# Batch 0's early attention pairs: v pooled by GpSimd, the pooled result kept on chip, key rows through DRAM left out

## The chip, the cores and the metric

The kernel runs on one core of a Trainium2 chip. The metric is the time of one execution in microseconds (us), and smaller is better. The engines are named as in the profile: PE multiplies matrices (its weight load is PEld), DVE and ACT are the vector and the scalar engine, POOL is GpSimd, and SP issues the transfers.

## What is computed

```python
# q, k, v: (8 batches, 8 heads, 576 positions, 64)
q_d, k_d, v_d = (t.reshape(B, H, 144, 4, D).mean(axis=3) for t in (q, k, v))
out_up = np.repeat(softmax(q_d @ k_d.T / 8) @ v_d, 4, axis=2)
mask = abs(i - j) < 4
out_local = softmax(where(mask, q @ k.T / 8, -1e9)) @ v
x = (out_up + out_local) as (batch, 576 positions, 512 channels)
u = x + ((x.T @ U @ V).T)              # U 576x32, V 32x576
out = u + relu(u @ w_ch1) @ w_ch2      # 512 -> 2048 -> 512
```

Two attentions are added: one over positions averaged in fours, whose result each position of a four receives, and one over a band of seven neighbours. A product of rank 32 mixes the positions, and a feed-forward part (FFN) follows. U, V and the two weight matrices arrive as 64-bit floats; the kernel splits each into a high and a low part, and each FFN product is three matrix products (high by high, high by low, low by high).

## The kernel before

The attention is cut into 32 pairs, a batch and two of its heads; pair n is heads 2(n mod 4) and the next one of batch n div 4. The FFN is cut into 256 steps: 8 batches, 2 tiles of 288 positions, 16 chunks of 128 hidden channels. A step has an `ffn1` (12 matmuls, L888: u by a chunk of w1 into `ps_h`) and an `ffn2` (12 matmuls, L911: the hidden chunk by w2 into `acc`), and `ffn2` runs three steps behind. u is held for a whole batch as `uH` and `uL`, 128 channels (one pair) by 288 positions each, so the FFN of a batch starts when the u of its fourth pair is there.

There are two ways to make a pair. The first NE = 5 pairs are early: `early_global` averages q and k on POOL, averages v by matmuls with the constant matrix `pool_sb` (L427), and writes the attention over averages to DRAM (`up_e`). `load_up` brings it back into rows 38 to 45 of `vw`, the tile with v's windows for the band. `local_blocks` computes the band in blocks of 32 positions on PE; its last product (`ps_ba`, L651) multiplies `vw`, and so contains the averaged part. `early_mix` makes u from the result `ob`: `hu` (L673) multiplies it by `Ublk`, and `um` adds V's product (L688) and turns the blocks by matmuls with the identity (L690). Pair 4 is early too, but belongs to batch 1: its x goes to DRAM (L661, L662).

The other pairs are late: `late_global`, then `local_attn`, where POOL forms the products `Pt` of the band (L795; five of them for a pair, the last half as wide) from tiles `vl` that are loaded for it, and DVE sums them (L800). x goes to DRAM, `mix_part` loads it (`xL`, `Y`), and u is made of `hu` (L844), V's product (L859), `uH` on ACT (L865) and `uL` on POOL (L867).

W1 and W2 are split by `convert`, 16 chunks each: ACT (L339), three DVE instructions (L341, L343, L345), ACT for the high part (L347), POOL for the low part (L350). W2's parts lie where the early pairs' tiles were, so no W2 chunk is finished before the last early operation is done (the key "late"). `load_ublk` and `load_v` split U and V in the same way.

Nothing waits at run time except for data and buffers: `Plan` is given every operation with an assumed duration and a priority, simulates the five engines, and writes the order of each engine's instructions once. An engine then runs its instructions in that order, so an instruction that waits holds back all behind it.

## Time and profile before

| | |
|---|---|
| time, median of 3 runs | 990.95 us (990.48 to 991.46) |
| profiled execution | 992.23 us, of which its trace spans 990.4 us |
| mean granted clock of PE | 0.972 of full speed |
| busy share of the span | PE 95%, POOL 55%, DVE 52%, ACT 39% |

The span runs from the first to the last instruction of the trace; the rest of the execution's time lies around it. Busy shares are means over stages that differ, so the stages have rows of their own further down.

### The profile page before, as it was taken

Reading aid. Unit: us, or ns where it says so; the run is one execution under the profiler, and the core shown is the slowest. Engines: PE = TensorE matmul, PEld = TensorE weight load, DVE = VectorE, ACT = ScalarE, POOL = GpSimd, SP = SyncE. Lnnn points to the kernel's source line nnn. Section 1 sums busy time; section 2 is a strip of 40 time slices with the busy share of each in tenths; the row PEclk is TensorE's granted clock in tenths of the full one; section 3 lists DMA queues with packets and bytes.
Section 4 is the critical chain, followed back from the end, with each engine's and each line's share of the span. In section 5 each row is a group of like instructions: output and inputs, shape, how many; then the busy total and the mean of one; then the engine's idle time right before and its main releaser. Section 6 shows DMA issues by size and latency. Waiting matters only on the chain.

```text
span 990.4 us, 26862 instructions
## 1 busy us (share of the span) xinstructions
...
## 2 busy tenths in 40 slices
...
GB/s 263 277 137 171 204 210 92 141 144 100 142 117 123 114 109 116 150 126 123 119 111 132 106 126 111 150 126 127 124 101 135 120 109 87 105 36 25 1 25 25
DMA packets 222612, 120.30 MB, mean 121 GB/s; under 512 B 175492, under 2 KB 198456, under 8 KB 222488
## 3 DMA queue, kind: packets, MB, share of 16 engines
...
q14 instruction: 39, 0.32, 0.1%
HBM read 87.78 MB, written 30.75 MB: 120 GB/s over the span
## 4 chain that ended last, share of the span: by engine, by line
PE 81%; DVE 11%; ACT 3%; issue 2%; DMA 2%; POOL 1%; SPq 0%; DVEq 0%; ACTq 0%; POOLq 0%
PE ps_h L888 34%; PE acc L911 34%; PE ps_a L548 3%; DVE acc L800 2%; PE ps_b L715 2%; DVE c L343 2%; PE ps_hu L844 1%; DVE o L925 1%; PE ps_t L535 1%; PE ps_v L427 1%; DVE c L345 1%; PE ps_b L722 1%; PE ps_a L480 1%; DVE hL L896 1%; DVE c L341 1%
## 5 line engine op out<-in xcount | busy, mean ns | idle before, releaser
L888 PE MATMUL ps_h<-uH,W1H 128*128 128x288 f32 x1024 | 297.9, 291 | 4.7 <-DVE hL L896 4.7
L911 PE MATMUL acc<-hH,W2H 128*128 128x288 f32 x1024 | 299.8, 293 | 0.0
L888 PE MATMUL ps_h<-uL,W1H 128*128 128x288 f32 x1024 | 295.0, 288 | 0.6 <-POOL uL L867 0.6
L888 PE MATMUL ps_h<-uH,W1L 128*128 128x288 f32 x1024 | 294.8, 288 | 0.0
L911 PE MATMUL acc<-hH,W2L 128*128 128x288 f32 x1024 | 293.6, 287 | 0.7 <-POOL W2L L350 0.7
L911 PE MATMUL acc<-hL,W2H 128*128 128x288 f32 x1024 | 293.3, 286 | 0.0
L896 DVE SCALAR_TENSOR_TENSOR hL<-ps_h,hH 128x288 fp32r<-128x288 f32 x256 | 116.5, 455 | 332.4 <-ACT hH L895 331.3
L795 POOL TENSOR_TENSOR Pt<-vl,at 128x896 f32<-128x896 f32 (+1 forms) x135 | 218.9, 1691 | 114.9 <-DVE acc L800 59.1
L895 ACT ACTIVATE hH<-ps_h 128x288 fp32r<-128x288 f32 x256 | 104.8, 409 | 350.6 <-PE ps_h L888 349.0
L888 PEld LDWEIGHTS ps_h<-uH,W1H 128*128 128x128 f32 x1024 | 195.3, 191 | 7.1 <-DVE hL L896 5.8
L888 PEld LDWEIGHTS ps_h<-uL,W1H 128*128 128x128 f32 x1024 | 195.4, 191 | 0.9 <-POOL uL L867 0.9
L888 PEld LDWEIGHTS ps_h<-uH,W1L 128*128 128x128 f32 x1024 | 195.4, 191 | 0.0
L911 PEld LDWEIGHTS acc<-hH,W2L 128*128 128x128 f32 x1024 | 194.0, 189 | 1.1 <-POOL W2L L350 1.1
L911 PEld LDWEIGHTS acc<-hH,W2H 128*128 128x128 f32 x1024 | 194.1, 190 | 0.4
L911 PEld LDWEIGHTS acc<-hL,W2H 128*128 128x128 f32 x1024 | 194.1, 190 | 0.0
L800 DVE TENSOR_REDUCE acc<-Pt 128x128 f32<-128x1024 f32 (+1 forms) x135 | 146.3, 1104 | 2.3 <-POOL Pt L795 1.4
L836 POOL TENSOR_TENSOR xL<-xL,xH 116x640 fp32r<-116x640 f32 x28 | 43.3, 1547 | 110.5 <-ACT xH L835 102.1
L921 POOL TENSOR_TENSOR o<-uH,uL 128x288 f32<-128x288 f32 x64 | 49.0, 796 | 49.5 <-DMA out_t<-o 49.5
L740 ACT ACTIVATE se<-ps_b 96x114 f32<-96x114 f32 x108 | 38.4, 355 | 73.1 <-PE ps_b L715 59.9
L506 POOL TENSOR_TENSOR vr<-vr 72x256 f32<-72x256 f32 x54 | 40.6, 753 | 30.3 <-DMA vr<-in_v 30.3
L867 POOL TENSOR_TENSOR uL<-xT,uH 128x288 fp32r<-128x288 f32 x56 | 43.7, 801 | 21.3 <-ACT uH L865 21.3
L789 ACT ACTIVATE Pt<-ul 128x128 f32<-128x128 f32 (+1 forms) x135 | 46.2, 421 | 14.0 <-DVE acc L800 13.7
(126 smaller groups left out, 1091.1 us busy)
## 6 DMA issues: line engine op xcount, KB each, us to landing
...
```

What stands on the lines that cost most here:

```text
L506: pool_tt(256, lambda x=x: nc.gpsimd.tensor_tensor(out=x()[:, :, 0:2, :], in0=x()[:, :, 0:2, :], in1=x()[:, :, 2:4, :], op=ALU.add), [x], ...
L740: act(n * KL, lambda p=ps[hh], se=se, n=n, rows=rows: nc.scalar.activation(se()[rows, 0:n].rearrange("p r k -> p (r k)"), p()[rows, 0:n * ...
L789: act(n * D, lambda n=n, ps=ps, Pt=Pt: nc.scalar.activation(Pt()[:, :n, :, 7], ul()[:, ps, :], AF.Copy), [ul], [(Pt, 1)], prio, 0.16)
L795: nc.gpsimd.tensor_tensor(out=Pt()[:, :n, :, 0:7].rearrange("p s d o -> p o s d"), in0=win, in1=at()[:, ps, :].rearrange("p s o -> p o s") ...
L800: dve(8.5 * n * D, lambda n=n, ps=ps, Pt=Pt: nc.vector.tensor_reduce(out=acc()[:, ps, :], in_=Pt()[:, :n], axis=AX.X, op=ALU.add), [(Pt, 0 ...
L836: pool_tt(640, lambda: nc.gpsimd.tensor_tensor(out=xL(), in0=xL().bitcast(F32), in1=xH().bitcast(F32), op=ALU.subtract), [xL, xH], [xL], prio)
L867: pool_tt(TN, lambda uH=uH, uL=uL, uf=uf: nc.gpsimd.tensor_tensor(out=uL()[:, hp, :], in0=uf(), in1=uH()[:, hp, :].bitcast(F32), op=ALU.su ...
L888: nc.tensor.matmul(ps()[:, :TN], w[:, dc, fs], turns(u()[:, dc, :]), start=(n == 0), stop=(n == 3 * NDC - 1))
L895: last_h[i] = act(TN, lambda: nc.scalar.activation(hH(), ps()[:, :TN], AF.Relu), [ps], [hH], FIRST, 0.05)
L896: dve(TN, lambda: nc.vector.scalar_tensor_tensor(hL(), ps()[:, :TN], 0.0, hH().bitcast(F32), op0=ALU.max, op1=ALU.subtract), [ps, hH], [hL ...
L911: nc.tensor.matmul(ac[e]()[:, :TN], W2[w][:, fc, es], turns(hx()), start=(fc == 0 and n == 0), stop=(fc == NFC - 1 and n == 2))
L921: pool_tt(TN, lambda e=e, o1=o1: nc.gpsimd.tensor_tensor(out=o1()[:, :TN], in0=uH()[:, e, :].bitcast(F32), in1=uL()[:, e, :].bitcast(F32), ...
```

## The change

NE becomes 4, so that the early pairs are those of batch 0 and pair 4 is made as a late pair. In the early pairs v is loaded in groups of four positions (`vre`, 72 partitions by 4 by 256) and averaged by two POOL additions. The attention over averages stays on chip: `od` is turned by two transposes (`o_mm`) into `ot`, which DVE adds to u with each value repeated four times (`uf`). Its share of x by U enters `hu` through `Upool`, U's block averaged by six matmuls once, and two more matmuls for each pair. The store to `up_e`, its load into `vw` and the constant rows that went with it (`pat_sb`) are gone. The blocks of `ob` are turned by three transposes per tile, ahead of V's product. `uH` and `uL` are made from `uf`, `uL` now on POOL. U's block and V are loaded with priority 0.6 in place of 1.5 and through buffers of the late pairs, `pool_sb` is loaded later, and late scores wait for the last early `hu`.

```diff
-    NE = 5
+    NE = 4
...
-    KU = KL + QL // 4
...
+    ring([NS, 2, KW], "ms_b")
+    ring([4, D], "vs_e")
+    ring([4, SD], "E_e")
+    ring([NL + 2, D], "vw", 2, NL)
+    dma(lambda: nc.sync.dma_start(out=pool_sb, in_=pool), [], ["pool"], 1.5, 74)
...
-        raw = early_raw("ur")
+        raw = raw_buf("ur")
+        pu = psum(ps_m, "ps_up", "m:x", 2)
...
+        def mm():
+            for n, (r, a) in enumerate(CROSS):
+                nc.tensor.matmul(view()[:, a], pool_sb[:, 64 - QL * r + QH * a:64 - QL * r + QH * a + QH], Ublk[:, r, :],
+                                 start=(n == 0), stop=(n == len(CROSS) - 1))
+        op(PE, 1.5, mm, ["UbH", "pool"], [pu], prio)
+        act(4 * R, lambda: nc.scalar.activation(Upool[:], view(), AF.Copy), [pu], ["Upool"], prio, 0.05)
...
-    def early_global(b, hp, up_s, prio, qt, kt, vn):
+    def early_global(b, hp, prio, qt, kt, vr):
...
-        v4 = lambda t: t()[:QH, :4 * D].rearrange("p (a h d) -> p a h d", a=2, h=2)
-
-        def v_mm():
-            for n, (r, a) in enumerate(CROSS):
-                nc.tensor.matmul(v4(pv)[:, a], pool_sb[:, 64 - QL * r + QH * a:64 - QL * r + QH * a + QH], vn()[:, r],
-                                 start=(n == 0), stop=(n == len(CROSS) - 1))
-        op(PE, pw(prio) * 2.4, v_mm, [vn, "pool"], [pv], prio)
...
-        op(PE, pw(prio) * 1.4, s_mm, [sq, sk], ps, prio)
+        op(PE, 0.9, s_mm, [sq, sk], ps, prio)
+        vs = ring([4, D], "vs_e")
+        pool_tt(512, lambda: nc.gpsimd.tensor_tensor(
+            out=vr()[:, :, 0:2 * D], in0=vr()[:, :, 0:2 * D], in1=vr()[:, :, 2 * D:4 * D], op=ALU.add), [vr], [vr], prio, 2.2)
+        pool_tt(256, lambda: nc.gpsimd.tensor_tensor(
+            out=vs()[:QH], in0=vr()[:, :, 0:D], in1=vr()[:, :, D:2 * D], op=ALU.add), [vr], [vs], prio, 2.2)
...
-        for hh in range(2):
-            dma(lambda hh=hh: nc.sync.dma_start(
-                out=up_s()[hh].rearrange("(a p) d -> p a d", a=2), in_=od()[:, 2 * hh:2 * hh + 2, :]),
-                [(od, hh)], [(up_s, hh)], prio, 40)
+        op(PE, 1.2, a_mm, ek + [vs], [pa], prio)
+        pt = psum(ps_m, "ps_o", "m:g", 2)
+
+        def o_mm():
+            for a in range(2):
+                nc.tensor.transpose(pt()[:, a * QH:(a + 1) * QH], od()[:, a].rearrange("p h d -> p (h d)"), ident_sb[:QH, :QH])
+        op(PE, 0.24, o_mm, [od, "ident"], [pt], prio)
+        ot = work(True, glo, [128, SD], F32, "ot")
+        act(SD, lambda: nc.scalar.activation(ot(), pt()[:, :SD], AF.Copy), [pt], [ot], prio)
+        return od, ot
...
-    def load_up(vw_t, up_s, prio):
-        for hh in range(2):
-            dma(lambda hh=hh: nc.sync.dma_start(
-                out=vw_t()[hh * KW + KL:hh * KW + KU, 0:NL],
-                in_=up_s()[hh].rearrange("(n j) d -> j n d", j=QL // 4)), [(up_s, hh), (vw_t, hh)], [(vw_t, 2 + hh)], prio, 40)
...
-                    o = slice(hh * KW, hh * KW + KU)
+                    o = slice(hh * KW, hh * KW + KL)
                     nc.tensor.matmul(av(pa[hh])[c * QL:(c + 1) * QL, r], et()[o, r, c * QL:(c + 1) * QL],
                                      vw_t()[o, n, :], start=(r == 0), stop=(r == NS - 1))
-        op(PE, pw(prio) * 2.2, a_mm, [(et, 0), (et, 3)] + [(vw_t, i) for i in range(4)], pa, prio)
+        op(PE, pw(prio) * 2.2, a_mm, [(et, 0), (et, 3), (vw_t, 0), (vw_t, 1)], pa, prio)
...
-            dma(lambda hh=hh: put(hh), [(ob, hh)], [(x_s, hh)], prio, 295, 0.9)
-
+    def early_mix(b, hp, x, od, ot, prio):
...
-                nc.tensor.matmul(ph()[:2 * R, :2 * D], Ublk[:, n, :], flat(n), start=(n == 0), stop=(n == NS - 1))
-        op(PE, pw(prio) * 2.0, hu, rd + ["UbH"], [ph], prio)
+                nc.tensor.matmul(ph()[:2 * R, :2 * D], Ublk[:, n, :], flat(n), start=(n == 0), stop=False)
+            for a in range(2):
+                nc.tensor.matmul(ph()[:2 * R, :2 * D], Upool[:, a, :], od()[:, a].rearrange("p h d -> p (h d)"),
+                                 start=False, stop=(a == 1))
+        op(PE, 1.8, hu, rd + ["UbH", "Upool", od], [ph, "early_hu"], prio)
...
-            op(PE, pw(prio) * 1.05, um, rd + [(stk, 0), (stk, 1), (stk, 2), "ident", "V0H", "V1H", "V0L", "V1L"], [pu], prio)
+            def xt(pu=pu, blocks=blocks):
+                for n, r in enumerate(blocks):
+                    nc.tensor.matmul(pu()[:, n * 128:(n + 1) * 128], flat(r), ident_sb, is_transpose=True,
+                                     start=(n == 0), stop=False)
+
+            def um(t=t, pu=pu, off=off):
+                nc.tensor.matmul(pu()[:, off:off + TN], stk(), Vst[:, t * TN:(t + 1) * TN], start=False, stop=True)
+            op(PE, 0.4, xt, rd + ["ident"], [pu], prio)
+            op(PE, 0.25, um, [pu, (stk, 0), (stk, 1), (stk, 2), "V0H", "V1H", "V0L", "V1L"], [pu], prio)
...
-            dve(TN, lambda uH=uH, uL=uL, pu=pu: nc.vector.tensor_tensor(
-                out=uL()[:, hp, :], in0=pu()[:, :TN], in1=uH()[:, hp, :].bitcast(F32), op=ALU.subtract),
-                [pu, (uH, hp)], [(uL, hp)], prio)
+            uf = work(True, mix, [128, TN], F32, "uf")
+            fold = lambda x: x.rearrange("p (j r) -> p j r", r=4)
+            dve(TN + 85, lambda t=t, pu=pu, uf=uf, off=off: nc.vector.tensor_tensor(
+                out=fold(uf()), in0=fold(pu()[:, off:off + TN]),
+                in1=ot()[:, t * QH:(t + 1) * QH].unsqueeze(2).broadcast_to([128, QH, 4]), op=ALU.add), [pu, ot], [uf], prio)
+            act(TN, lambda uH=uH, uf=uf: nc.scalar.activation(uH()[:, hp, :], uf(), AF.Copy),
+                [uf], [(uH, hp)], prio, 0.12)
+            pool_tt(TN, lambda uH=uH, uL=uL, uf=uf: nc.gpsimd.tensor_tensor(
+                out=uL()[:, hp, :], in0=uf(), in1=uH()[:, hp, :].bitcast(F32), op=ALU.subtract),
+                [uf, (uH, hp)], [(uL, hp)], prio)
...
-        op(PE, 1.1, mm, [qr, kr, sq, sk], ps, prio)
+        op(PE, 1.1, mm, [qr, kr, sq, sk, "early_hu"], ps, prio)
...
-                up_s = buf(dram, [2, SD, D], F32, "up_e", bufs=2)
-                early_global(b, hp, up_s, p, qt, kt, load_vn(b, 2 * hp, p))
-                load_up(vw_t, up_s, p)
...
-                    x_s = buf(dram, [2, S, D], F32, "x_s", bufs=6)
-                    local_blocks(b, hp, x_s, qt, kt, vw_t, p + 1)
-                    held.append((b, hp, x_s, p + 2))
...
+                od, ot = early_global(b, hp, p, qt, kt, load_vr(b, 2 * hp, p))
+                x = local_blocks(b, hp, qt, kt, vw_t, p + 1)
+                if hp == 0:
+                    load_ublk(p + 0.6)
+                    load_v(p + 0.6)
+                early_mix(b, hp, x, od, ot, p + 2)
...
-    for h in held:
-        mix_part(*h)
-    attention(1, False)
```

The first place is PE's order around the first pair's last band product (`ps_ba`). Before, three other pairs' scores (`ps_b`) and averages of v stand ahead of it, and this follows:

```order
L596 MATMUL ps_b<-kd,qt 32x38 x36
L440 MATMUL ps_s<-smk,smq 72x144 x4
L651 MATMUL ps_ba<-vw_108,et 32x64 x40
L639 MATMUL ps_bt<-ident_sb,ms_b_99 128x128 x5
L673 MATMUL ps_hu<-ob,Ublk 64x128 x5
L688 MATMUL ps_u<-Vst,stk 128x288
L690 MATMUL ps_u<-ident_sb,ob 128x128 x2
```

With the change it stands behind the scores of the first two pairs alone:

```order
L583 MATMUL ps_b<-kd,qt 32x38 x36
L466 MATMUL ps_a<-vs_e_102,E_e_106 72x64 x8
L626 MATMUL ps_bt<-ident_sb,ms_b_98 128x128 x5
L477 MATMUL ps_o<-ident_sb,od 128x72 x2
L638 MATMUL ps_ba<-vw_110,et 32x64 x40
L421 MATMUL ps_s<-smk,smq 72x144 x4
L653 MATMUL ps_hu<-ob,Ublk 64x128 x5
L655 MATMUL ps_hu<-od,Upool 64x128 x2
L671 MATMUL ps_u<-ident_sb,ob 128x128 x3
```

The band product has moved from PE's 47th row to its 18th, and the turning of `ob` stands ahead of V's product.

The second place is PE's order at the boundary between the FFN of batch 0 (`ffn2` of its last step) and that of batch 1. Before, the `hu` of one late pair, pair 7, stands there:

```order
L911 MATMUL acc_2668<-hH,W2L 128x288
L844 MATMUL ps_hu<-xH,Ust 64x128 x5
L844 MATMUL ps_hu<-xL,Ust 64x128 x5
L859 MATMUL ps_u<-Vst,stk 128x288 x2
L888 MATMUL ps_h<-uH,W1H 128x288
```

With the change those of pairs 6 and 7 stand there, and work of pairs 9 and 10 between them:

```order
L901 MATMUL acc_2563<-hH,W2L 128x288
L834 MATMUL ps_hu<-xH,Ust 64x128 x5
L834 MATMUL ps_hu<-xL,Ust 64x128 x5
L849 MATMUL ps_u<-Vst,stk 128x288 x2
L540 MATMUL ps_a<-vs,E 72x64 x8
L712 MATMUL ps_b<-smk,smq 32x144 x4
L712 MATMUL ps_b<-smk,smq 8x144 x2
L705 MATMUL ps_b<-gT,gq 32x38 x30
L712 MATMUL ps_b<-smk,smq 32x144 x4
```

They end with eight transposes (`ps_t`), pair 7's `hu` and V's products, and the first `ffn1` of batch 1. The `hu` of pair 6 has moved behind the whole FFN of batch 0.

The third place is POOL's order up to the last `uL` of batch 1, which is the last row of both pieces. Before, pair 8's products `Pt` stand just ahead of it:

```order
L795 TENSOR_TENSOR Pt<-vl,at 128x7x128
L867 TENSOR_TENSOR uL<-xT,uH 128x288 x3
L836 TENSOR_TENSOR xL<-xL,xH 116x640
L795 TENSOR_TENSOR Pt<-vl,at 128x7x128 x2
L795 TENSOR_TENSOR Pt<-vl,at 128x7x64
L867 TENSOR_TENSOR uL<-xT,uH 128x288 x2
```

With the change:

```order
L785 TENSOR_TENSOR Pt<-vl,at 128x7x128 x4
L826 TENSOR_TENSOR xL<-xL,xH 116x640
L785 TENSOR_TENSOR Pt<-vl,at 128x7x64
L498 TENSOR_TENSOR vr<-vr 72x2x128
L500 TENSOR_TENSOR vs<-vr 72x128
L857 TENSOR_TENSOR uL<-xT,uH 128x288 x2
```

Between the last low part of W2 and this last `uL` POOL has 14 whole and 4 half `Pt` before, and 18 whole and 5 half ones with the change: pair 4's have been added, and pair 8's still stand ahead.

## Rows read from the trace of the kernel before

**Rows 1.** The windows view: the span cut into six stages. Columns: the stage, its length, busy time of each engine with its count of instructions, granted clock of PE, busy share of the DMA engines, GB/s.

```profile
0.00:82.50 82.50, 58.86 (x1023) 49.77 (x1024) 54.29 (x120) 46.78 (x146) 44.96 (x56) 0.83 0.75 218
82.50:118.00 35.50, 26.64 (x427) 24.03 (x425) 24.08 (x46) 22.43 (x64) 14.48 (x13) 0.76 0.69 177
118.00:163.40 45.40, 39.21 (x496) 37.63 (x494) 43.29 (x63) 24.16 (x62) 33.34 (x30) 1.00 0.68 194
163.40:221.70 58.30, 56.67 (x560) 56.35 (x560) 37.03 (x70) 24.28 (x81) 42.31 (x42) 0.97 0.53 126
221.70:230.30 8.60, 4.78 (x26) 3.75 (x26) 7.19 (x11) 1.86 (x6) 8.60 (x9) 0.79 0.23 72
230.30:990.40 760.10, 751.46 (x8309) 745.46 (x8308) 351.93 (x712) 269.86 (x877) 396.23 (x422) 1.00 0.45 104
```

**Rows 2.** The timeline of PE: the first FFN matmul, and one at the start of batch 1's FFN. Columns: start, duration, engine, line, operation, written and read tiles; in brackets the idle time before it and what ended that.

```profile
82.52 0.37 PE L888 MATMUL ps_h<-uH,W1H 128*128 128x288 f32 x1
...
229.64 0.61 PE L888 MATMUL ps_h<-uL,W1H 128*128 128x288 f32 x1 [0.56 <-POOL uL L867]
```

**Rows 3.** Groups of PE's instructions from 0 to 240 us, of the early pairs' steps that the diff touches. Columns: line, engine, operation, shapes, count, busy time, mean ns of one, idle time before and what ended it.

```profile
L427 PE MATMUL ps_v<-vn,pool_sb 128*72 128x128 f32 x60 | 12.6, 393 | 3.6 <-DMA pool_sb<-in_pool 3.6
L480 PE MATMUL ps_a<-vs_e,E_e 128*72 128x64 f32 x80 | 10.1, 292 | 3.7 <-ACT E_e L473 3.6
L690 PE MATMUL ps_u<-ident_sb,ob 128*128 128x128 f32 (+3 forms) x48 | 7.3, 296 | 0.0
L440 PE MATMUL ps_s<-smk,smq 64*72 64x144 f32 x40 | 6.1, 350 | 0.6 <-DVE uL L696 0.5
L673 PE MATMUL ps_hu<-ob,Ublk 128*64 128x128 f32 x40 | 5.9, 300 | 0.2 <-ACT E_e L455 0.2
L639 PE MATMUL ps_bt<-ident_sb,ms_b 128*128 128x128 f32 x25 | 3.8, 282 | 1.2 <-ACT ob L655 1.2
```

**Rows 4.** Groups of DVE's instructions from 82.5 to 163.4 us: the three instructions of a W2 chunk.

```profile
L345 DVE SCALAR_TENSOR_TENSOR c<-w2r,c 128x512 int32<-128x512 int32 x16 | 16.0, 1003 | 0.2
L343 DVE SCALAR_TENSOR_TENSOR c<-w2r,c 128x512 int32<-128x512 int32 x16 | 14.5, 906 | 0.2
L341 DVE TENSOR_SCALAR c<-c 128x512 int32<-128x512 int32 x19 | 13.7, 719 | 7.7 <-ACT c L339 7.7
```

**Rows 5.** The timelines of SP, ACT, POOL and DVE around the first W2 chunks, in this order: pair 4's stores of x, the first high parts, the first low parts, two DVE instructions of W2 chunks.

```profile
97.82 1.24 SPq L661 DMA_DIRECT2D x_s<-ob  x1
101.94 0.52 SPq L662 DMA_DIRECT2D x_s<-ob  x1
106.77 1.67 ACT L347 ACTIVATE W2H<-c 128x512 fp32r<-128x512 f32 x3
107.47 3.72 POOL L350 TENSOR_TENSOR W2L<-c,W2H 128x512 fp32r<-128x512 f32 x3 [8.80 <-DMA up_s<-od]
101.64 0.43 DVE L341 TENSOR_SCALAR c<-c 128x512 int32<-128x512 int32 x1 [2.36 <-ACT c L339]
111.37 0.43 DVE L341 TENSOR_SCALAR c<-c 128x512 int32<-128x512 int32 x1 [4.33 <-ACT c L339]
```

**Rows 6.** The timeline of POOL from the last low part of W2 to the last `uL` of batch 1.

```profile
162.07 1.34 POOL L350 TENSOR_TENSOR W2L<-c,W2H 128x512 fp32r<-128x512 f32 x1
...
179.30 5.26 POOL L795 TENSOR_TENSOR Pt<-vl,at 128x896 f32<-128x896 f32 x3 [2.40 <-DMA vl<-in_vp]
...
195.99 0.79 POOL L867 TENSOR_TENSOR uL<-xT,uH 128x288 fp32r<-128x288 f32 x1 [5.32 <-ACT uH L865]
196.75 7.88 POOL L795 TENSOR_TENSOR Pt<-vl,at 128x896 f32<-128x896 f32 x5
...
210.93 0.80 POOL L867 TENSOR_TENSOR uL<-xT,uH 128x288 fp32r<-128x288 f32 x1 [3.24 <-ACT uH L865]
...
224.45 4.47 POOL L795 TENSOR_TENSOR Pt<-vl,at 128x896 f32<-128x896 f32 x3
228.76 1.58 POOL L867 TENSOR_TENSOR uL<-xT,uH 128x288 fp32r<-128x288 f32 x2
```

**Rows 7.** The timeline of SP: two loads of a late pair's v tiles. Columns: time of issue, length of the issue, queue, line, operation, tiles.

```profile
174.53 1.18 SPq L704 DMA_DIRECT2D vl<-in_vp  x2
...
188.05 1.12 SPq L704 DMA_DIRECT2D vl<-in_vp  x2
```

**Rows 8.** The chain of work that ended last, in order of time (start, length, engine, tile, line): two pieces of later pairs' attention inside batch 0's FFN.

```profile
193.59 1.03 PE ps_a L548 x16
...
198.54 0.68 PE ps_b L715 x51
```

**Rows 9.** Groups of POOL's instructions from 0 to 100 us, of one shape each: the nearest to v's averaging.

```profile
L506 POOL TENSOR_TENSOR vr<-vr 72x256 f32<-72x256 f32 x3 | 2.8, 932 | 0.0
```

**Rows 10.** One line's group from 0 to 240 us: `uL` on POOL.

```profile
L867 POOL TENSOR_TENSOR uL<-xT,uH 128x288 fp32r<-128x288 f32 x8 | 6.3, 807 | 10.4 <-ACT uH L865 10.4
```

**Rows 11.** POOL and DVE side by side: the timelines of a low part of W1 and of the DVE instruction that runs beside it, then of one at 113.79 us, when POOL is idle; last the durations of W2's L345 over the whole trace (least, median and greatest, in ns; first and last start in us).

```profile
93.02 1.70 POOL L350 TENSOR_TENSOR W1L<-c,W1H 128x512 fp32r<-128x512 f32 x1 [1.29 <-ACT W1H L347]
93.61 1.66 DVE L345 SCALAR_TENSOR_TENSOR c<-w2r,c 128x512 int32<-128x512 int32 x1
113.79 0.68 DVE L345 SCALAR_TENSOR_TENSOR c<-w2r,c 128x512 int32<-128x512 int32 x1
L345 DVE SCALAR_TENSOR_TENSOR c<-w2r,c x16: 677/746/1656, 93.6 to 159.6; 128x512 int32<-128x512 int32 x16
```

141 lines of the change are left out of this document (46 added, 95 removed).

## The prediction, made blind

> **What bounds the kernel now.** I read the stages first [rows 1]. From 230.3 us on PE is busy 751.46 of 760.1 us: the end comes 760.1 us after the last `uL` of batch 1, and nothing but PE's own work counts there. Ahead of it PE idles for 44 us (the idle of the first five stages: 23.6, 8.9, 6.2, 1.6 and 3.8), so what the change can give or take is when that last `uL` comes.
>
> Three waits stand in a row up to it. Until 82.5 us PE makes the early pairs, 58.86 busy of 82.5, and the first FFN matmul starts at 82.52 [rows 1, 2]. Then batch 0's FFN waits for W2 chunks, whose splitting is DVE's: from 118.0 to 163.4 us DVE is busy 43.29 of 45.4, that is 95% [rows 1], and the last W2 low part ends at 162.07 + 1.34 = 163.4 [rows 6]. From there to the end of the last `uL`, 228.76 + 1.58 = 230.3, POOL works through the `Pt` of pairs 5 to 8 [rows 6]. PE's order has pair 7's `hu` behind the whole FFN of batch 0, and the reader is to see in rows 2 that an `ffn1` matmul of batch 1 waits for that `uL` on POOL (idle 0.56). So the span is T2 + X + R: 163.4 for the last W2 part, 66.9 from there to the last `uL`, 760.1 for the rest.
>
> **T1, the end of the early phase (82.5 before).** PE's work there: v's averages go, −12.6; the identity matmuls, 7.3 for 48, become 24 transposes, which at the price of the 25 of `ps_bt` (3.8) are −3.5; two more matmuls per pair in `hu` are 16 records, since the rows count an fp32 matmul twice (L427 has 60 for 5 times 6), and at 5.9/40 that is +2.4; the transposes of `od` and Upool's matmuls, 8 and 12 records at 0.15, +3.0; pair 4's share, a fifth of `ps_s` (6.1) and half a fifth of `ps_a` (10.1) since part of it stands later, −2.2 [rows 3]. 58.9 − 12.9 = 46.0. Idle was 82.5 − 58.9 = 23.6. The 3.6 in front of v's averages, for `pool_sb`, go with these; the 3.7 in front of `ps_a`, for ACT, may go or stay [rows 3]. Idle is 16.3 to 23.6; I take 19, as one wait surely goes and part of the other. The band product of the first pair has moved from row 47 to row 18 of PE's order, since it no longer waits for a trip through DRAM, and that speaks for the low half. T1 = 65 (62 to 70).
>
> **T2, the last W2 part.** From 82.5 to 163.4, 80.9 us, DVE was busy 24.08 + 43.29 = 67.4 [rows 1]. By the order 10 W1 chunks are done by the end of the early pairs and not 13, so three more stand in this stretch, at 0.719 + 0.906 + 1.003 = 2.63 each [rows 4]: +7.9, to 75.3. The 13.5 of idle hold a gate: no W2 chunk could be written before pair 4's x was stored, at 101.94 [rows 5]; the first high parts follow at 106.77, and DVE idles 2.36 and 4.33 for buffers that ACT could not give back [rows 5]. With pair 4 late there is no such store, and the early tiles are free when the last early u is made. I let these two go and keep the rest, 6.8. 75.3 + 6.8 = 82.1, T2 = 65 + 82 = 147. Without any gain from the gate and at the late end of T1 it is 70 + 88.8 = 159; with T1 = 62 and 3 us less idle, 141.
>
> **X, from the last W2 part to the last `uL` of batch 1.** Here the change costs. POOL has 14 whole and 4 half `Pt` in this stretch before and 18 and 5 after: pair 4's five are added, with their sums, loads, `xL` and `uL`, and pair 8's still stand ahead of the last `uL`. A pair took 188.05 − 174.53 = 13.5 us from load to load [rows 7], and 196.75 − 179.30 = 17.4 from its first `Pt` to the next one's [rows 6]: its `vl` tiles have one buffer each, so the next load comes when POOL has read them. I take 15: X = 82. The boundary gives the same: batch 0's FFN ended 58.3 us after T2 [rows 1], hence at 205, and behind it now stand two pairs' `hu`, 8.6 as before [rows 1] and one period of 13.5 to 17.4 more, which is 227 to 231, where 147 + 82 is 229. If the two waits for `uH` (5.32 and 3.24, [rows 6]) go, because PE now waits less in front of them, X falls to 73; with the long period it is 84.
>
> **R, the rest.** Two pieces of attention, 1.03 of `ps_a`, 0.68 of `ps_b` and some 0.5 of the other half of `ps_b`, which stood inside the FFN of batch 0 [rows 8] and have their like at the boundary, where PE waits anyway, take 2.2 off what comes later: 757.9. Bounds: nothing gained, 760.1, and 756. The new additions on POOL (v's averages, `uL`) lie in the first 82 us, where it was busy 44.96 [rows 1]; two of v's per pair at 932 ns for 256 elements, the first twice as long, are 2.8, [rows 9], and 8 `uL` at 807 ns are 6.5 [rows 10], together 18 us less the averages of pair 4. There is room for it, 37 us idle; what it costs if it delays DVE is rival A. The 8 `uf` on DVE replace 7 `uL` there and an eighth later, at one price; the load of v in another shape takes the place of the load of its rows, and both hide behind the first scores. The wait of late scores for the last early `hu` costs nothing, as both are PE's and stand in that order in its queue. U's block and V, split through three shared buffers in place of one, can only come earlier; what they take from DVE ahead of the first scores is their own 6 instructions or so, which were there before.
>
> **Sum.** 147 + 82 + 757.9 = 986.9 of span. The profiled execution lasted 1.8 more than its span, 992.23, but the median of the runs is 0.55 above the span, and I add that: 987.4 us, 3.5 less than 990.95. The bounds are 141 + 73 + 757 = 971 and 159 + 84 + 760 = 1003. The change breaks even where T2 + 82 + 757.9 is 990.4, at T2 = 150.5: 3.5 us of lost time up to there.
>
> **Rivals.**
> *A, slower: POOL's new work blocks DVE.* A POOL subtraction of two SBUF tiles at 93.02 took 1.70 and the DVE instruction beside it 1.66; the same instruction took 0.68 with POOL idle, and over all W2 chunks its least, median and greatest are 677, 746 and 1656 ns [rows 11]. So up to 1 us is lost for each meeting. T2 is a sum of DVE's work: with 16 to 18 us more on POOL and 10 to 14 DVE instructions beside it, it loses 10 to 14 us before T1 or behind it: T2 = 157 to 161, and 997 to 1001 in time. From 3.5 us on, four meetings, the gain is gone. Against it: much of the new POOL work falls where DVE waits for PE anyway (DVE was busy 54.29 of 82.5 [rows 1]). The Trainium skill has a rule that speaks for this rival: in "SBUF — State Buffer", section "Who interferes with whom", a DVE instruction with two SBUF inputs contends with a GpSimd instruction that reads SBUF, and whoever is second blocks for as long as the other holds the port; the trace agrees with its 0.68 and 1.66.
> *B, slower: the early phase is no shorter.* PE, in its order, waits for GpSimd's v instead of for its own matmuls, and T1 stays near 82: T2 = 82 + 82 = 164, time 1004. For it: POOL is in order too, and v's averages stand between those of q and k; against it, 12.6 us of matmuls are gone whatever waits.
> *C, faster: X is short.* With PE free earlier, `hu` and `uH` are ready when POOL asks, and a pair costs the 13.5 or less; X = 72 to 75, time 977 to 980. For it: 8.6 us of waits in rows 6; against it, with one buffer of `vl`, the idle of 2.40 before the load at 179.30 comes in every period.
>
> **How the numbers follow.** Main case, T2 near 147 and X near 82: 0.50; A 0.20, B 0.10, C 0.20. The main case's own range is 981 to 993, from T1's 62 to 70 and the period's 13.5 to 17.4. A change within 0.2% (2 us, about what the measurement of this kernel can tell) is 989 to 993. Of the main case 0.32 lies below that, 0.14 in it and 0.04 above; A gives 0.05 to "same" and 0.15 to slower, B 0.10 to slower, C 0.20 to faster: faster 0.52, same 0.19, slower 0.29. The range reaches to C's middle and into A: 975 to 999; it leaves out B, A's last third and C's best.
>
> **What would show it.** In the trace of after: the first FFN matmul between 62 and 70; the last low part of W2 between 141 and 152; no idle time of DVE for L339 above 2 us in the stretch of W2; POOL's last `uL` of batch 1 80 to 84 us behind the last W2 part; and PE waiting 20 us or more at the boundary of batches 0 and 1. A shows as L345 and L343 above 1 us on average with T2 past 155, B as a first FFN matmul past 75 with PE waiting for POOL's v, C as an X below 76. I am wrong altogether if PE is busy less or more than 750 to 758 us behind that `uL`, for then the rest moved too.

## The result, and the profile after

The change made the kernel slower: 998.32 us (median of 10 runs, 992.40 to 1002.21) against 991.21 (10 runs); the ratio is 1.0069, 95% interval 1.0049 to 1.0089. The forecast was 987.4, 3.5 us faster, with a range of 975 to 999. The profiled execution lasted 1000.12 us with a span of 998.3, a little above the median.

The windows view of after, cut at the same events as [rows 1]: the first FFN matmul (73.3), 118, the last low part of W2 (163.8), 210, the last `uL` of batch 1 (245.5).

```profile
0.00:73.30 73.30, 51.90 (x968) 42.54 (x968) 55.19 (x101) 40.83 (x127) 50.07 (x63) 0.82 0.69 199
73.30:118.00 44.70, 32.85 (x422) 30.10 (x415) 32.92 (x62) 26.83 (x82) 29.43 (x30) 0.81 0.71 195
118.00:163.80 45.80, 39.09 (x461) 37.33 (x460) 36.16 (x58) 24.00 (x60) 27.03 (x23) 0.89 0.62 173
163.80:210.00 46.20, 44.81 (x472) 44.22 (x472) 31.41 (x58) 20.35 (x71) 38.17 (x39) 1.00 0.60 140
210.00:245.50 35.50, 20.14 (x214) 17.68 (x213) 20.34 (x36) 13.38 (x44) 26.33 (x24) 0.64 0.58 141
245.50:998.30 752.80, 748.65 (x8191) 742.72 (x8189) 348.89 (x708) 264.17 (x857) 390.51 (x414) 1.00 0.44 103
```

The sum T2 + X + R, before against after: T2 163.4 and 163.8, X 66.9 and 81.8 (245.5 − 163.8), R 760.1 and 752.8. X is what was forecast (82). The early phase ended 9.2 us earlier, T1 73.3 against 82.5, but the last W2 part did not come earlier at all. R fell by 7.3 and not by 2.2. PE's work in it fell by 2.8 (from 751.46 to 748.65, and from 8309 PE instructions to 8191), since some of it now stands ahead of the joint, where PE idles 15.4 us between 210 and 245.5. The other 4.5 are idle time. Before, PE waited five times behind the joint for DVE's `hL`; in after it does not (us, times, longest, from 230.3 us on):

```profile
PE ps_h L888 <- DVE hL L896: 4.7, 5, 0.9
```

No run shows what took these waits away.

Where T2's stretch went shows in DVE's groups from 73.3 to 163.8 us of after, which answer to [rows 4]. Columns as there:

```profile
L331 DVE SCALAR_TENSOR_TENSOR c<-w2r,c 128x512 int32<-128x512 int32 x16 | 16.7, 1047 | 0.2
L329 DVE SCALAR_TENSOR_TENSOR c<-w2r,c 128x512 int32<-128x512 int32 x16 | 15.0, 935 | 0.2
L327 DVE TENSOR_SCALAR c<-c 128x512 int32<-128x512 int32 x21 | 11.7, 556 | 12.0 <-ACT c L325 12.0
```

DVE is busy 32.92 + 36.16 = 69.1 of 90.5 us and idles 21.4, of which 12.0 in front of a chunk's first instruction, for ACT; 4.2 more are for PE's `ps_a` and 2.1 for ACT's `se`, both of late pairs. What ACT waited for is in the view of the tile `w2r` (over the whole trace: us, times), and what the loads of W2 waited for in SP's queue from 73.3 to 163.8 (us, times, longest):

```profile
DMA w2r<-in_W: 13.0, 7
SPq L385 <- DVE c L331: 14.8, 6, 6.5
```

The first was 3.5 us, once, before; the second was 13.7 us, 8 times, so the loads waited for a buffer in both kernels. The chunks go round a loop: DVE's third instruction (L331) frees one of three raw buffers, the next load goes out, lands, ACT reads it, DVE waits for ACT.

The end of POOL's chain in after answers to [rows 6]; pair 8's `Pt` again stand ahead of the last `uL`:

```profile
162.43 1.33 POOL L336 TENSOR_TENSOR W2L<-c,W2H 128x512 fp32r<-128x512 f32 x1
...
176.29 5.27 POOL L785 TENSOR_TENSOR Pt<-vl,at 128x896 f32<-128x896 f32 x3 [1.23 <-DVE lrl L766]
...
191.40 6.96 POOL L785 TENSOR_TENSOR Pt<-vl,at 128x896 f32<-128x896 f32 x4 [1.04 <-DMA vl<-in_vp]
...
240.14 1.02 POOL L785 TENSOR_TENSOR Pt<-vl,at 128x448 f32<-128x448 f32 x1
...
243.98 1.55 POOL L857 TENSOR_TENSOR uL<-xT,uH 128x288 fp32r<-128x288 f32 x2 [1.69 <-ACT uH L855]
```

And the chunk instructions of the early phase, DVE's groups of after from 0 to 73.3 us, then of before from 0 to 82.5:

```profile
L329 DVE SCALAR_TENSOR_TENSOR c<-w1r,c 128x512 int32<-128x512 int32 x11 | 11.7, 1066 | 0.3
L327 DVE TENSOR_SCALAR c<-c 128x512 int32<-128x512 int32 x11 | 11.3, 1032 | 4.2 <-ACT c L325 4.1
L331 DVE SCALAR_TENSOR_TENSOR c<-w1r,c 128x512 int32<-128x512 int32 x10 | 9.7, 976 | 0.1
```

```profile
L345 DVE SCALAR_TENSOR_TENSOR c<-w1r,c 128x512 int32<-128x512 int32 x13 | 10.8, 827 | 0.2
L343 DVE SCALAR_TENSOR_TENSOR c<-w1r,c 128x512 int32<-128x512 int32 x13 | 9.8, 757 | 0.2
L341 DVE TENSOR_SCALAR c<-c 128x512 int32<-128x512 int32 x14 | 7.1, 510 | 2.5 <-ACT c L339 2.5
```

A chunk cost DVE 3.07 us in place of 2.09 (2.73 in the second trace of after, e15). The first W1 load went out at 13.1 us in place of 6.1, as U's block and V hold the buffers first, and the first chunk's last DVE instruction started at 28.4 in place of 17.0. By the ninth chunk this was made up: its last DVE instruction started at 65.2 us before and at 65.1 after. For the tenth and the sixteenth it is, before and then after,

```profile
70.27 0.68 DVE L345 SCALAR_TENSOR_TENSOR c<-w1r,c 128x512 int32<-128x512 int32 x1
...
90.87 1.41 DVE L345 SCALAR_TENSOR_TENSOR c<-w1r,c 128x512 int32<-128x512 int32 x1
```

```profile
70.45 0.68 DVE L331 SCALAR_TENSOR_TENSOR c<-w1r,c 128x512 int32<-128x512 int32 x1
...
91.89 1.65 DVE L331 SCALAR_TENSOR_TENSOR c<-w1r,c 128x512 int32<-128x512 int32 x1
```

and for the last 159.6 and 159.9. In between the chunks of after fall behind (W2's first: 93.6 and 98.4) and catch up. At these marks the stream of 32 chunks came at the same times on the clock, within about 1 us, and the early phase ended at another place in it.

### The profile page after: what moved, and what is told of

It reads as the page before. It is cut to its first block, busy times and chain, and to the rows that moved or that the text cites. A ratio compares the mean times of both kernels' runs of the same rounds, so it can differ in the third digit from the quotient of the medians.

```text
span 998.3 us, 26648 instructions
## 1 busy us (share of the span) xinstructions
PE 937.4 (94%) x10712; PEld 914.6 (92%) x10712; DVE 524.9 (53%) x1020; ACT 389.6 (39%) x1239; POOL 561.5 (56%) x589
## 4 chain that ended last, share of the span: by engine, by line
PE 82%; DVE 7%; DMA 4%; issue 2%; ACT 2%; SPq 1%; POOL 1%; DVEq 0%; ACTq 0%; POOLq 0%
PE acc L901 35%; PE ps_h L878 35%; PE ps_a L540 3%; PE ps_b L705 2%; DVE c L329 2%; DMA w2r<-in_W 2%; PE ps_hu L834 2%; DVE c L331 1%; PE ps_t L527 1%; PE ps_b L712 1%; PE ps_u L849 1%; DVE o L915 1%; DVE c L327 1%; DVE acc L790 1%; DMA vre<-in_v 1%
## 5 line engine op out<-in xcount | busy, mean ns | idle before, releaser
L785 POOL TENSOR_TENSOR Pt<-vl,at 128x896 f32<-128x896 f32 (+1 forms) x140 | 227.0, 1688 | 83.4 <-DVE acc L790 54.5
L790 DVE TENSOR_REDUCE acc<-Pt 128x128 f32<-128x1024 f32 (+1 forms) x140 | 151.1, 1103 | 1.6 <-POOL Pt L785 0.6
L826 POOL TENSOR_TENSOR xL<-xL,xH 116x640 fp32r<-116x640 f32 x28 | 43.3, 1546 | 100.7 <-ACT xH L825 74.3
L779 ACT ACTIVATE Pt<-ul 128x128 f32<-128x128 f32 (+1 forms) x140 | 48.8, 422 | 34.6 <-DVE acc L790 30.3
```

Of the source, the lines that this page charges most:

```text
L779: act(n * D, lambda n=n, ps=ps, Pt=Pt: nc.scalar.activation(Pt()[:, :n, :, 7], ul()[:, ps, :], AF.Copy), [ul], [(Pt, 1)], prio, 0.16)
L785: nc.gpsimd.tensor_tensor(out=Pt()[:, :n, :, 0:7].rearrange("p s d o -> p o s d"), in0=win, in1=at()[:, ps, :].rearrange("p s o -> p o s") ...
L790: dve(8.5 * n * D, lambda n=n, ps=ps, Pt=Pt: nc.vector.tensor_reduce(out=acc()[:, ps, :], in_=Pt()[:, :n], axis=AX.X, op=ALU.add), [(Pt, 0 ...
L826: pool_tt(640, lambda: nc.gpsimd.tensor_tensor(out=xL(), in0=xL().bitcast(F32), in1=xH().bitcast(F32), op=ALU.subtract), [xL, xH], [xL], prio)
```

## The experiments

A row for each kernel: the marks of its trace (us) and its time against the kernel before on the same chip. S is the sum of DVE's instructions on the 32 chunks, from the groups of L341, L343 and L345 (L327, L329 and L331 after) or their rows. The two traces of the kernel after differ by 3.7 us in T2, so the traces tell places, and the ratios tell times.

| kernel | T1 | S | T2 | X | R | span | ratio (95%) |
|---|---|---|---|---|---|---|---|
| before | 82.5 | 78.2 | 163.4 | 66.9 | 760.1 | 990.4 | 1 |
| after | 73.3 | 86.1 | 163.8 | 81.8 | 752.8 | 998.3 | 1.0069 (1.0049 to 1.0089) |
| e1 | 82.2 | 77.9 | 155.9 | 82.5 | 752.5 | 990.9 | 1.0032 (1.0014 to 1.0050) |
| e2 | 75.0 | 84.0 | 159.8 | 82.1 | 752.5 | 994.4 | 1.0059 (1.0040 to 1.0079) |
| e3 | 91.4 | 84.9 | 151.6 | 86.4 | 765.2 | 1003.2 | 1.0158 (1.0132 to 1.0185) |
| e4 | 74.2 | 87.1 | 166.7 | 64.2 | 760.8 | 991.6 | 1.0027 (1.0008 to 1.0047) |
| e5 | 80.9 | 82.7 | 163.1 | 67.6 | 759.7 | 990.4 | 1.0044 (1.0022 to 1.0066) |
| e6 | 86.2 | 86.3 | 158.0 | 82.5 | 751.8 | 992.3 | 1.0087 (1.0056 to 1.0118) |
| e7 | 75.6 | 83.7 | 157.7 | 82.8 | 753.4 | 993.9 | 1.0092 (1.0057 to 1.0127) |
| e8 | 74.6 | 88.3 | 162.2 | 83.0 | 752.5 | 997.6 | 1.0090 (1.0056 to 1.0125) |
| e9 | 93.3 | 87.2 | 152.2 | 86.5 | 765.1 | 1003.8 | 1.0177 (1.0144 to 1.0210) |
| e10 | 92.9 | 85.5 | 149.4 | 77.3 | 766.4 | 993.2 | 1.0068 (1.0040 to 1.0096) |
| e11 | 88.8 | 78.0 | 152.5 | 82.7 | 764.8 | 1000.0 | 1.0136 (1.0104 to 1.0168) |
| e12 | 71.9 | 87.9 | 157.4 | 88.5 | 751.8 | 997.7 | 1.0119 (1.0086 to 1.0152) |
| e13 | 71.2 | 79.4 | 156.6 | 81.8 | 753.4 | 991.8 | 1.0064 (1.0042 to 1.0086) |
| e14 | 74.3 | 91.6 | 164.6 | 67.0 | 755.5 | 987.1 | 0.9978 (0.9965 to 0.9990) |
| e15 (after again) | 74.7 | 82.9 | 160.1 | 81.8 | 753.2 | 995.1 | 1.0062 (1.0043 to 1.0081) |
| e16 | 74.5 | 86.5 | 156.6 | 82.0 | 751.7 | 990.2 | 1.0018 (1.0002 to 1.0034) |
| e17 | 75.7 | 83.0 | 157.9 | 81.7 | 753.3 | 993.0 | 0.9994 (0.9974 to 1.0015) |

**e1, one number of the change alone.**

```diff
-    NE = 5
+    NE = 4
```

> The kernel before with one number changed: NE is 4, so that pair 4 is made as a late pair; v's averaging, the way through DRAM and all else stay. Terms: T2 is the end of the last low part of W2, X the time from there to the last uL of batch 1, R the rest. Theory S (the 32 chunks of W1 and W2 are one stream through three shared buffers, which sets T2 whenever the early pairs end): T2 stays at 161 to 166 although no store of pair 4's x stands ahead of W2, X goes from 66.9 to about 82, R to about 753, span 996 to 1002. Theory G (the prediction's: T2 follows the end of the early pairs and the gate in front of W2): T2 falls to 150 to 157, span 985 to 993.

T2 fell by 7.5, X rose by 15.6, R fell by 7.6: the time rose by 0.3%. The windows of e1, cut at T1, T2 and the last `uL`:

```profile
0.00:82.20 82.20, 56.36 (x1005) 47.40 (x1005) 55.96 (x117) 46.92 (x146) 46.77 (x56) 0.79 0.70 218
82.20:155.90 73.70, 65.55 (x783) 62.36 (x783) 61.24 (x105) 43.61 (x119) 46.58 (x42) 0.95 0.64 178
155.90:238.40 82.50, 65.72 (x773) 62.74 (x774) 53.36 (x94) 34.00 (x116) 67.12 (x68) 0.84 0.65 155
238.40:990.90 752.50, 748.36 (x8191) 742.36 (x8189) 348.82 (x708) 264.54 (x857) 390.65 (x412) 1.00 0.44 102
```

T2 is theory G's (150 to 157), but not by its mechanism. From T1 to T2 DVE was busy 67.4 and idle 13.5 us before ([rows 1]), and is busy 61.2 and idle 12.5 in e1: 6.2 us of its work left that stretch, and the idle time that I had put down to the gate stayed: DVE's waits for ACT in front of a chunk were 7.7 us in four, the longest 4.3, and are 7.7 us in seven, the longest 1.5. X and R are those of the whole change, as theory S had them. In after DVE is busy 69.1 and idle 21.4 there: the rest of the change ends the early phase 8.9 us earlier and adds 7.9 of DVE's work and 8.9 of its idle time behind it.

**e4 and e5, what holds a late pair's products.** In `local_attn`:

```diff
-        for p0 in range(0, NPOS, 2):
-            n = min(2, NPOS - p0)
-            Pt = buf(loc, [128, 2, D, 8], F32, "Pt", "Pt", 3)
+        own = b * HP + hp < 6
+        step = 1 if own else 2
+        for p0 in range(0, NPOS, step):
+            n = min(step, NPOS - p0)
+            Pt = buf(loc, [128, step, D, 8], F32, "Pt", "Ph" if own else "Pt", 1 if own else 3)
...
```

> The kernel after, with the products Pt of pairs 4 and 5 in a small buffer of their own (one position instead of two, nine products per pair) in place of the three buffers that they share with the raw chunks of W1 and W2. Theory P (pair 4's products stand behind T2 only because the W2 chunks hold those buffers, not because GpSimd is full: it is idle 19 of 46 us from 118 to 163.8): products of pair 4 start near 100 to 120, X falls by a pair or more, to 60 to 70, and the time is 980 to 988, unless they slow DVE: they may lengthen its chunk instructions by up to 1 us each and T2 by 4 to 8. If GpSimd's or DVE's work is itself what fills the time, X falls by what T2 rises, and the time stays at 996 to 1000.

> The kernel before with NE 4 and, as in the run on the kernel after, the products Pt of pairs 4 and 5 in a small buffer of their own. The NE 4 kernel alone had T2 155.9, X 82.5, R 752.5, span 990.9. Theory P (the late pair is on the path only because its products wait for the buffers of the W2 chunks): T2 157 to 161 from more work beside DVE, X 60 to 68, R 758 to 761 as the FFN then starts with less of later pairs' attention done, span 979 to 987. Its rival, that the time is filled by GpSimd's and DVE's work whatever the buffers: span 989 to 993.

In POOL's timeline of e4 pair 4's products now start long before T2 (156.39 in after):

```profile
92.88 1.39 POOL L787 TENSOR_TENSOR Pt<-vl,at 128x448 f32<-128x448 f32 x1 [1.50 <-DVE at L768]
...
103.60 1.24 POOL L787 TENSOR_TENSOR Pt<-vl,at 128x448 f32<-128x448 f32 x1
```

X fell by 17.6 in e4 and 14.9 in e5, as theory P said: `Pt` and the raw chunks share three buffers, the chunks have the lower priority number, and a late pair's products wait for the last chunks. The times did not follow: 993.1 us in e4, between the two forecasts (980 to 988 and 996 to 1000), and a span of 990.4 in e5, which is the rival's. On the kernel after the buffer is worth 0.4%; on NE 4 alone nothing, as T2 came 7.2 later and R rose by as much. In both, R has the five waits for `hL` again, 4.7 us.

**e2, e6, e7: parts of the change.** e2 is after with the early `uL` on DVE and v's additions replaced by a copy; e6 and e7 add one part each to e1. The main lines:

```diff
+            act(256, lambda: nc.scalar.activation(vs()[:QH], vr()[:, :, 0:D], AF.Copy), [vr], [vs], prio)   # e2
...
+        raw = raw_buf("ur")        # e6, and "vraw"; priority p + 0.6
...
+        pool_tt(512, ...)          # e7: v's two additions, no v_mm
+        pool_tt(256, ...)
```

> The kernel after without its new work on GpSimd: the early uL is made by DVE again, and v's two additions are left out (ACT copies the first row of each four instead, so the averaged attention uses wrong values of v; the time of the rest is what counts). Theory C (GpSimd's new work blocks DVE's three instructions per chunk, which are 0.98 us longer per chunk up to 73 us): those instructions fall back to 0.5 to 0.85 us in that stretch, T2 comes 6 to 11 us earlier and the time is 987 to 992. Theory S (the stream through three buffers): the first FFN matmul may come a few us earlier, but chunk 8 and all later ones stay within 2 us, T2 is 162 to 165, and the time 996 to 1000.

> The kernel before with NE 4 and one more part of the change: the raw U block and V are loaded first and into the three buffers of the W1 chunks. Theory H (this holds up the stream of chunks at its start, and the stream does not make it up): the first chunk's last DVE instruction starts near 25 to 30 us in place of 16, the sum of DVE's chunk instructions stays near 78 us, T2 is 159 to 164, X near 82, the span 994 to 999. Theory C (only GpSimd's new work beside DVE slows the stream): T2 stays at 154 to 158, the span at 989 to 993.

> The kernel before with NE 4 and another part of the change alone: v is averaged by two GpSimd additions per early pair in place of the matmuls; the way through DRAM stays. Theory C: eight additions of 1.3 and 0.7 us beside DVE lengthen its chunk instructions, whose sum rises from 77.9 to 80 to 84 us, and T2 comes 2 to 5 us later, 158 to 161, although 12.6 us of matmuls are gone; the span is 992 to 997. Theory H: the sum stays, T2 falls with PE's work to 151 to 155, and the span is 985 to 990.

Either part alone, on e1, lengthens S, by 8.4 and 5.8 us, and costs 0.55 to 0.6% of time by the medians, with intervals that overlap that of the whole change. In e7, which came near theory C's numbers, the first FFN matmul came 6.6 us earlier and the time still rose. e6 has no new work on GpSimd and the same S as after, where theory H had 78: an S above 78 is not GpSimd's new work alone. e2, without that work, has S 84.0, 2.68 us for a chunk up to T1 and no time that its interval tells from that of after: the time (996.2) is theory S's, T2 (159.8) lies between the two.

**e3 and e9 to e12: more parts, taken out of after.** e3: own buffer for the raw U and V. e9: that, and their priority as before. e10: e9 with v by matmuls (and so v loaded by rows and `pool_sb` first, as before). e11: e10 with the early `uL` on DVE. e12: after with v by matmuls. The main lines:

```diff
-        raw = raw_buf("ur")
+        raw = early_raw("ur")                      # e3, e9, e10, e11, and "vraw"
...
-                    load_ublk(p + 0.6)
+                    load_ublk(p + 1.5)             # e9, e10, e11, and load_v
...
+        op(PE, pw(prio) * 2.4, v_mm, [vr, "pool"], [pv], prio)   # e10, e11, e12
...
+            dve(TN, lambda uH=uH, uL=uL, uf=uf: nc.vector.tensor_tensor(   # e11
```

> The kernel after with the raw U block and V in a buffer of their own again, as before, so that they don't hold the three buffers of the W1 chunks at the start: the first W1 load goes out near 6 us and not at 13.1. If the stream's late start is what it never makes up (theory S, first form), all chunks come 5 to 7 us earlier, T2 is 157 to 159 and the time 991 to 994. If the stream catches up whatever its start, because from chunk 8 on it is paced by what happens after 60 us (theory S, second form), T2 is 162 to 165 and the time 996 to 1000.

> The kernel after with U's block and V loaded with their former priority, 1.5, and in a buffer of their own; v by GpSimd and the on-chip result stay. The former run with the buffer alone kept the new priority. Theory A (each part's cost adds up: NE 4 alone +0.3%, U and V in the chunk buffers +0.55%, v by GpSimd +0.6%, the on-chip result the rest, about -0.75%): the time is 990 to 993, T2 155 to 160. Theory B (the parts delay the stream of chunks over the same stretch and don't add up): T2 161 to 165, the time 995 to 999. In both the first chunk's last DVE instruction starts near 16 us.

> As the run with U and V as before, and v averaged by matmuls of PE again: what is left of the change is NE 4, the pooled result kept on chip, the transposes and the early uL on GpSimd. Theory A: time 983 to 987, T2 148 to 154, the sum of DVE's chunk instructions 76 to 80 us. Theory B: 990 to 994, with T2 at 154 to 158 as in NE 4 alone, since the way through DRAM was never what the chunks waited for.

> As the run with the on-chip result alone, and the early uL made by DVE as before the change. Eight subtractions move from GpSimd (0.81 us each) to DVE (0.45 us each). Theory C (work on GpSimd costs DVE as much as it runs beside it): DVE's chunk instructions lose 2 to 4 us and DVE gains 3.6 us of its own work, so T2 and the time stay within 2 us of that run. If GpSimd's uL costs more than its share, T2 falls by 3 us or more.

> The kernel after with v averaged by PE's matmuls again, and U and V still in the chunk buffers with the new priority. Theory A: 0.6% less than the kernel after, 990 to 993, T2 156 to 160, DVE's chunk instructions 82 to 84 us in sum, T1 76 to 80 as PE has its 10 us of matmuls back. Theory B: T2 161 to 165, time 996 to 999.

None of the five went as either theory had it; parts can't be priced one by one here, since the planner orders each kernel anew. What they show together is a trade: with U and V out of the chunks' buffers the first W1 load goes out early, T2 falls to 149 to 153, but T1 rises to 89 to 93 and R to 765. In e9 PE has 753.9 us of work behind the joint (748.65 in after) and idles 11.2 there (4.2). I take it that DVE's time goes either to the chunks or to the early pairs; no run shows that by itself. The windows of e9, up to T1 and from the last `uL`:

```profile
0.00:93.20 93.20, 54.66 (x968) 44.27 (x968) 73.91 (x121) 48.66 (x139) 63.20 (x69) 0.72 0.67 193
...
238.70:1003.80 765.10, 753.90 (x8317) 747.31 (x8316) 357.60 (x723) 271.60 (x884) 398.56 (x423) 1.00 0.44 104
```

**e8, the loads' queue.**

```diff
-        dma(lambda: nc.sync.dma_start(out=raw(), in_=w2.bitcast(I32)[f * 128:(f + 1) * 128, :]),
+        op(ACT, 0.1, lambda: nc.scalar.dma_start(out=raw(), in_=w2.bitcast(I32)[f * 128:(f + 1) * 128, :]),
```

> The kernel after with the sixteen loads of W2 issued by ACT's queue in place of SP's. In the kernel after ACT waits 13.0 us for W2's raw chunks (3.5 before), and some loads stand in SP's queue behind stores of the late pairs that wait for DVE (the loads at 106.13 and 113.29 us). If SP's order is what holds the stream from 73 us on, T2 falls by 3 to 8 us, to 156 to 161, X stays near 82, and the time is 990 to 995. If the loads wait for a free buffer anyway, T2 stays within 2 us and the time at 997 to 1000.

No gain: T2 162.2 and 999.4 us, as the second forecast had it. SP's order is not what holds the stream. That the loads wait for a free buffer instead is what after's SP queue shows above (14.8 us for L331).

**e13, e15, e16, e17: one cause at a time in one order.** These keep every engine's order of instructions. e13 thins GpSimd's new work, e16 shortens W2's loads, e17 does both, e15 is after itself. The main lines:

```diff
-            out=vr()[:, :, 0:2 * D], in0=vr()[:, :, 0:2 * D], in1=vr()[:, :, 2 * D:4 * D], op=ALU.add)
+            out=vr()[:, :, 0:8], in0=vr()[:, :, 0:8], in1=vr()[:, :, 2 * D:2 * D + 8], op=ALU.add)
...
-                out=uL()[:, hp, :], in0=uf(), in1=uH()[:, hp, :].bitcast(F32), op=ALU.subtract),
+                uL()[:, hp, :].bitcast(F32), 0.0),                          # gpsimd.memset; e13, e17
...
-        dma(lambda: nc.sync.dma_start(out=raw(), in_=w2.bitcast(I32)[f * 128:(f + 1) * 128, :]),
+        dma(lambda: nc.sync.dma_start(out=raw()[:, :CN // 2], in_=w2.bitcast(I32)[f * 128:(f + 1) * 128, :CN // 2]),   # e16, e17
```

> The kernel after with every engine's instructions in the same order, but GpSimd's new ones made small: v's two additions work on 8 columns of 512 and 256, and the early uL is a memset, which reads nothing (so v's averages and the low part of batch 0's u are wrong, and only the time counts). Nothing is replanned, so what moves is contention and waiting for GpSimd alone. Theory C: the chunk instructions up to 73 us fall from 1.02 us to 0.75 to 0.9 on average, T2 comes 4 to 8 us earlier (156 to 160), X stays at 81 to 83, and the time is 0.4 to 0.8% below the kernel after. Theory O (the order of the instructions holds the stream back: which chunk stands behind which late pair's store): T2 stays within 2 us of 163.8 and the time within 0.2%.

> The kernel after, unchanged, on the same chip as the two others, so that they can be set against it: 996 to 1000, T2 162 to 165, X 81 to 83.

> The kernel after with every engine's instructions in the same order and of the same size, but each of the sixteen W2 loads brings a quarter of its chunk (128 KB in place of 512), and the splitting reads that quarter four times (so W2 is wrong; only the time counts). In the kernel after DVE idles 12.0 us from 73 us on for ACT, which waits 13.0 us for these loads. Theory L (the three buffers form a loop of load, ACT, DVE, and the loads' time is what the stream waits for): ACT's wait for W2's loads falls below 4 us, T2 comes 5 to 10 us earlier (153 to 157), and the time falls to 988 to 993. Theory D (DVE's work and its meetings with GpSimd fill the time): T2 stays within 3 us of 160 to 164.

> The quarter-size W2 loads and the thinned new GpSimd work together, in the same order of instructions (v's averages, the low part of batch 0's u and W2 are wrong; only the time counts). If each takes its own part of the stream's time, T2 is 148 to 153 and the time 984 to 990, which is where the prediction had it. If they hide each other, T2 is that of the better of the two alone.

DVE's groups on the chunks up to 165 us, of e13 and then of e15; the five busy times add up to S:

```profile
L327 DVE TENSOR_SCALAR c<-c 128x512 int32<-128x512 int32 x32 | 20.8, 651 | 18.7 <-ACT c L325 18.7
L329 DVE SCALAR_TENSOR_TENSOR c<-w2r,c 128x512 int32<-128x512 int32 x16 | 16.4, 1027 | 0.2
L331 DVE SCALAR_TENSOR_TENSOR c<-w2r,c 128x512 int32<-128x512 int32 x16 | 14.8, 925 | 0.2
L331 DVE SCALAR_TENSOR_TENSOR c<-w1r,c 128x512 int32<-128x512 int32 x16 | 14.0, 880 | 0.1
L329 DVE SCALAR_TENSOR_TENSOR c<-w1r,c 128x512 int32<-128x512 int32 x16 | 13.4, 839 | 0.3
```

```profile
L327 DVE TENSOR_SCALAR c<-c 128x512 int32<-128x512 int32 x32 | 22.2, 696 | 13.9 <-ACT c L325 13.8
L331 DVE SCALAR_TENSOR_TENSOR c<-w2r,c 128x512 int32<-128x512 int32 x16 | 16.5, 1034 | 0.2
L329 DVE SCALAR_TENSOR_TENSOR c<-w1r,c 128x512 int32<-128x512 int32 x16 | 15.3, 959 | 0.3
L331 DVE SCALAR_TENSOR_TENSOR c<-w1r,c 128x512 int32<-128x512 int32 x16 | 14.7, 921 | 0.1
L329 DVE SCALAR_TENSOR_TENSOR c<-w2r,c 128x512 int32<-128x512 int32 x16 | 14.2, 890 | 0.2
```

Between these two traces S, T1 and T2 all differ by 3.5 us, so that the stretch from T1 to T2 is 85.4 in both. After's first trace has T2 3.7 later than e15, with S 3.2 larger: one kernel differs from itself by as much as e13 from it. Within one order, with the loads as they are, T2 − S is 77.2 to 77.7. T2 (156.6) is where theory C had it, but by the timed runs e13 is not to be told from the kernel after (1.0064 and 1.0062). e16 is: 1.0018, and its interval ends below that of after. ACT's wait for W2's loads, in the view of `w2r` of e16, is

```profile
DMA w2r<-in_W: 1.7, 2
```

in place of 13.0 (7.3 in e15). That wait, T2 (156.6) and the time (991.9 us) are all theory L's. With both taken away the time (989.9) is by its interval not to be told from that of the kernel before (0.9994), and T2, 157.9, is no better than with the loads alone; its profiled execution, 994.87, was one of its slowest. So W2's loads are worth some 0.45% in after's order. GpSimd's new work is worth something between nothing (e13) and a quarter of a per cent (e17 against e16), and neither is clear of the noise. The kernel before has such loads and GpSimd work of its own, and no run took them away there; that the two add up to what the change cost does not show that the change brought them.

**e14, v by matmuls and the small buffer together.** e12's matmuls for v and e4's small buffer, on the kernel after.

> The two edits together that moved T2 and X: v averaged by PE's matmuls (T2 157.4 there, but X 88.5), and the products Pt of pairs 4 and 5 in a small buffer of their own (X 64.2 there). If the two act apart from each other: T2 158 to 162, X 62 to 68, R 758 to 761, span 980 to 988, faster than both kernels. If what leaves the path is made up by the work beside it, as in NE 4 with the buffer: T2 163 to 167 and the span 989 to 994.

It took 988.90 us against 990.72 of the kernel before and 997.01 of the kernel after on the same chip: 0.2% less than before, by an interval that ends at 0.9990. X is 67.0 as hoped, T2 164.6 is not. Its windows, cut at T1, T2 and the last `uL`:

```profile
0.00:74.30 74.30, 55.95 (x1016) 46.58 (x1016) 54.20 (x104) 43.89 (x133) 43.46 (x56) 0.87 0.68 203
74.30:164.60 90.30, 71.48 (x801) 65.74 (x792) 81.56 (x133) 51.49 (x151) 66.83 (x62) 0.90 0.69 189
164.60:231.60 67.00, 58.06 (x744) 56.25 (x744) 44.23 (x82) 26.51 (x90) 55.33 (x61) 0.93 0.62 148
231.60:987.10 755.50, 751.32 (x8218) 745.24 (x8208) 352.74 (x711) 270.15 (x877) 392.19 (x416) 1.00 0.45 104
```

From T1 to T2 DVE is busy 81.56 of 90.3 where it had 69.1 of 90.5 in after. Late pairs' sums take 9.4 us there (1.2 in after), the chunk instructions 4.9 more, and DVE's wait for ACT in front of a chunk falls from 12.0 to 5.1: the sums stand where DVE had waited. That is the gain: the same T2, with a pair's products done in front of it.

## Why the prediction was wrong

The frame held: T2 + X + R, with the last `uL` of batch 1 as the joint, describes both traces. Term by term:

- **X was right**: forecast 82, measured 81.8, and 82.5 in e1. The main case's price of a late pair, 15 us, is shown by e1, and e4 shows what it depends on: the shared buffers, which the prediction did not name. Rival C (X of 72 to 75) was wrong.
- **R** fell by 7.3 where 2.2 was forecast. PE's work behind the joint fell by 2.8, near the forecast; the other 4.5 is idle time. The prediction read that nothing but PE's own work counts there, but 8.6 us of R were idle before, 4.7 of them waits for `hL`.
- **T1**: 73.3 for 65. PE was busy 51.9 where the sum of rows had 46.0, and idle 21.4 where it had 19. The sum had no term for the scores of the first late pair, which PE makes from 70.85 to 73.32 us, ahead of the first FFN matmul (before, none stand there). And the rows' prices did not carry over: `hu`'s 40 matmuls took 8.2 us in place of 5.9, and the 24 transposes 4.9 in place of 3.8, while PE's granted clock was 0.62 from 60 to 73.3 us (0.94 from 60 to 82.5 before). The prediction also put U's block and V in the chunks' buffers at nothing; with a buffer of their own (e3) T1 is 91.4, T2 151.6 and R 765.2.
- **T2 is the step that failed**: 163.8 for 147. The prediction added 82 us behind T1: 75.3 of DVE's work and 6.8 of idle time. DVE's work was less, 69.1; the idle time was 21.4. With T1's 8.3 that is 8.3 − 6.2 + 14.6 = 16.7, the whole error. In the second trace of the same kernel, e15, the idle time is 15.4 and the sum 9.7 − 5.3 + 8.6 = 13.0. So the idle time is the term that was mis-sized, by 8.6 to 14.6 us, beside T1. The stretch from T1 to T2 in e15, and then in e16, which differs in W2's loads alone (a quarter of the size, and read four times by the splitting):

```profile
74.70:160.10 85.40, 68.02 (x878) 64.09 (x873) 70.03 (x120) 50.56 (x142) 57.27 (x52) 0.89 0.71 195
74.50:156.60 82.10, 67.20 (x879) 63.56 (x874) 72.94 (x120) 50.30 (x142) 58.16 (x52) 0.89 0.52 126
```

  With short loads DVE idles 9.2 us in place of 15.4, nearly all of the difference in front of a chunk, for ACT (4.0 in place of 9.9), and the stretch is in sum the 82 that was forecast. Two assumptions made the error. One is that the stretch runs at DVE's pace. The stream runs through three raw buffers, and DVE idles for their loads where no other work fills the time; the 95% that I read as DVE's bound [rows 1] was the second half of the stretch alone, over the whole it was 83% (67.4 of 80.9). The other is that the gate's two waits (2.36 and 4.33, [rows 5]) would go with the gate. e1 took the gate away: the long waits went, and shorter ones of the same sum took their place.
- **Rival A** (GpSimd blocks DVE) has its mechanism in the rows: 0.43 and 0.68 us for chunk instructions with GpSimd idle ([rows 5], at 111.37, and [rows 11]), 1.03 and 1.07 on average for L327 and L329 in the first 73.3 us. Its price was too high: 10 to 14 us forecast, 3.5 in e13's trace, which is no more than two traces of after differ, and not to be told in the timed runs. Its time, 997 to 1001, holds the measured one, but by another cause: that is luck. The Trainium skill, "SBUF — State Buffer", section "Who interferes with whom", names `tensor_scalar` among the instructions that can take the port shared with GpSimd. The trace agrees in that L327, a `tensor_scalar` with one input, took 1032 ns on average in after's early phase, where GpSimd was busy 50.07 of 73.3 us, against 0.43 us with GpSimd idle.
- **Rival B** (T1 no earlier) did not happen, but its T2 did, 164, by another road.

Of the signs named in advance, X's 80 to 84 us came. T1, T2 and DVE's idle time for ACT lie outside theirs, PE waited 15.4 us at the boundary and not 20, and its 748.65 us of work behind the last `uL` are below the 750 to 758 that were set as the bounds. By its own terms (T1 of 62 to 70, a period of 13.5 to 17.4) the main case's range would also be 983 to 995, and not 981 to 993.

What stays open is why ACT waits longer for the loads with the change, and how much of that is the loads' flight and how much the order in which planner and buffers let them go: e16 took 0.45% with loads a quarter as large, and e8's other queue took nothing. The kernel before was not run with short loads.
